# An output store that waits for a two-tap transfer to land, in a dynamic convolution with a tanh-shrink MLP behind it

## The chip, the cores and the metric

One core of one Trainium2 chip. The metric is device time in microseconds of one execution of the whole kernel, from inputs in HBM to the output in HBM. Engines are named TensorE (PE in the profile), VectorE (DVE), ScalarE (ACT), GpSimd (POOL) and SyncE (SP, which here only issues transfers).

## What is computed

The reference, cut to what matters. A softmax over 7 taps gives each token and head its own short filter; the filter runs causally over x; the result goes through two matrix products with `h - tanh(h)` between them.

```python
# x (8, 4096, 192), weight_gen (8, 4096, 8 heads, 7 taps), w_in (192, 2048), w_out (2048, 192), all float32
w = exp(weight_gen - max); w = w / sum(w)                     # over the 7 taps
x_pad = concatenate([zeros(B, 6, D), x], axis=1)              # causal: 6 rows of zeros ahead
x_unf = x_pad[:, idx, :].reshape(B, S, 7, H, D // H)
conv = einsum('bshk,bskhg->bshg', w, x_unf).reshape(B * S, D)
h = conv @ w_in
out = (h - tanh(h)) @ w_out                                   # (32768, 192)
```

## The kernel before, in words

The 32768 tokens are cut into 32 groups of 1024 tokens (128 partitions by 8 tokens). Everything is written out by hand in program order (a manual schedule); each engine runs its own instructions in that order and waits on semaphores for what it needs. The main loop runs over **bodies** n = 1 to 31. A body has 16 steps, f = 0 to 15, and does for different groups at once:

- TensorE: the first product of group n (`gemm1(n, f)`, line 584, tile `ph`), the second product of group n-1 in pieces (`out_pairs`, line 653, tiles `obank`), and in steps 13 and 14 the transposes of group n+1 (`transposes` and `conv_sums`, line 524, tile `pc`), which also add up those tap products that are still separate.
- ScalarE: tanh (line 597), the copies of finished output blocks to `out_sb` (`store_out`, line 672; two buffers), the exponentials (line 202).
- VectorE: `h - tanh(h)` (line 598, tile `gt`), and the small softmax work.
- GpSimd: the tap products of group n+2 (`products`, line 297). Taps 0 to 3 go into tile `pa` (three buffers), taps 4 to 6 into tile `pb` (one buffer).

The taps are added up by accumulating transfers from SBUF to SBUF that GpSimd issues (`dma_sum`, line 286). For groups 10 to 31 there are two: the **first sum** adds `pb`'s three taps to three of `pa` (`pa<-pb`, 1152 KB). Then the **second sum** adds taps 2 and 3 of `pa` to taps 0 and 1 (`pa<-pa`, 768 KB), the two-tap transfer of this case. The transposes then read only taps 0 and 1. GpSimd's order is: first sum of group m, `pa` products of group m+1, second sum of group m, `pb` products of group m+1, first sum of group m+1, and so on. The second sum of group n+1 comes in body n, in `products(n + 2)`, which is called at f = 1.

`LOCKED` names groups whose first sum has a further condition: its place in the program is step `LOCK` = 10 of the body two ahead of its group (`rest()`, line 954), and it waits for VectorE's subtraction of that step (`last_sub`).

SyncE issues the rest in program order, one queue: in body n the load of x for group n+3 (line 172, into `x_ring`; 1344 KB for an even group, 768 KB for an odd one), which waits until GpSimd has read the old rows; the **output store** of group n-2 (line 676, 768 KB), whose last block is finished by ScalarE at the end of f = 1; in bodies 9, 13, 17, 21 and 25 a small transfer that writes 6 rows of zeros at a sequence's start (line 182, `x_ring<-zero`, 4.5 KB), which waits for the x load of that body; and the load of weight_gen for group n+5 (line 161, 224 KB), which the exponential in body n+1 reads. From body 9 on the x load stands ahead of the store in the program.

A transfer's landing raises a semaphore, and whoever reads its bytes waits for that on its own engine. `order(inst, other, reason)` (line 144) makes one instruction wait for another, where `other` may be a transfer: then the wait is for its landing.

Of the kernel before, what the change touches and what calls it, by code (L numbers as in the profile page):

```python
# [16 lines left out]
def kernel(  # L17
# [8 lines left out]
    nc = tc.nc  # L26
# [25 lines left out]
    EXTRA_NORM = False  # L52

    WG_AT = 11
    LOCK, LOCKED = 10, tuple(range(15, 32))
    WARM = 0
    SUM_LATE = ()
    SUM_BEHIND = ()
# [19 lines left out]
    X3_AT = 3  # L78
    X3_BEHIND = None
    HALF = ()  # L80
    WOUT_CAST = ()
    SKEW = 6
    TAPS1 = ((True, 0, 1, 0, 8), (True, 1, 2, 0, 8), (False, 4, 6, 0, 8), (False, 6, 7, 0, 8), (False, 2, 4, 0, 8))
# [56 lines left out]
    tap_of = {}  # L140
    pace_of = {}
    sum_of = {}

    def order(inst, other, reason):
        tc.add_manual_dep(
            inst.ins,
            other.ins.name,
            mybir.DependencyInfo(mybir.DependencyClass.Sync, mybir.DependencyReason.DATA),
            reason=reason,
        )  # L150
# [3 lines left out]
    def tokens(t, n):  # L154

        m = n // 2
        return t[2 * m * TOK : 2 * (m + 1) * TOK].rearrange("(p s j) ... -> p s j ...", p=P, j=J)[:, n % 2]
# [127 lines left out]
    def dma_sum(out, in_):  # L285
        return nc.gpsimd.dma_start(  # L286
            out=out.rearrange("p k j d -> p k (j d)"),
            in_=in_.rearrange("p k j d -> p k (j d)"),
            accum_op=mybir.AluOpType.add,
            max_dma_last_dim=2 * J * D,  # L290
        )
# [65 lines left out]
    def products(n, taps=None, sums=None, hooks={}):  # L357
# [28 lines left out]
        def parts(*ks):  # L386
            return [[prod(k, k + 1)[:, 0] for k in ks]] * NC
# [27 lines left out]
        for k0, k1 in zip(cuts, cuts[1:]):  # L415
            if n - 1 in SUM2_EARLY and k0 == end - 1:
                second_sum(n - 1)
            m = most(k0, k1)
            if first is None and n - 1 in sum_of:
                sum_of.pop(n - 1)()  # L420
            first = first or m
        x_after[n + 1] = first
        second_sum(n - 1)
        def rest():
            a = PART_FILL.get(n, 0)
# [14 lines left out]
            else:  # L440
# [19 lines left out]
                if n in TWO_SUMS:  # L460
                    to_sum[n] = pa
                    prods_of[n] = parts(0, 1)
                elif n in HALF:
                    to_sum[n] = pa
# [3 lines left out]
                if n == NTOT - 1:  # L468
                    second_sum(n)
                    third_sum(n)  # L470
# [9 lines left out]
    def second_sum(n):  # L480

        if n in to_sum:
            pa = to_sum.pop(n)
            pairs = 1 if n in HALF else 2
            dma_sum(pa[:, 0:pairs], pa[:, 2 : 2 + pairs])
            if n in THREE or n in SINGLE:
                whole[n] = pa

# [150 lines left out]
    def out_stream():  # L639

        for i in range(LAST + 1):
            ops = []
            for r, blk in ((0, i), (1, i - 1)):
                if not 0 <= blk < LAST:
                    continue
                n, j = divmod(blk, J)
                if r == 0:
                    half[blk] = obank[blk % 2]
                ops.append((r, n, j, half[blk]))
            for f in range(NFT):  # L650
                for r, n, j, po in ops:
                    col = (j % 2) * HT + (j // 2) * P
                    mm = nc.tensor.matmul(  # L653
                        po[:, 0:D],
                        lhsT=g_of[n][f][r * R : (r + 1) * R, col : col + P],
                        rhs=w_out[r * R : (r + 1) * R, f, :],
                        start=(r == 0 and f == 0),
                        stop=(r == 1 and f == NFT - 1),
                    )
                    if r == 1 and f == 0 and i in (1, LAST):  # L660
                        order(mm, probe[0] if i == 1 else last_act[0], "row tiles in one bank")
                if f == NFT - 1 and i > 0:
                    store_out(i - 1)
                yield

    def store_out(blk):
        n, j = divmod(blk, J)
        po = half.pop(blk)
        if j == 0:
            out_of[n] = opool.tile([P, J, D], FP32, name="out_sb")  # L670
        out_sb = out_of[n]
        last_act[0] = nc.scalar.activation(out=out_sb[:, j, :], in_=po[:, 0:D], func=ACT.Copy)  # L672
        if j == J - 1:
            out_of.pop(n)
            g_of.pop(n)
            nc.sync.dma_start(
                out=tokens(out, n),
                in_=out_sb[:],
            )

    pairs = out_stream()

# [132 lines left out]
    if SOFT_EARLY:  # L815
# [6 lines left out]
        sums=SUMS1,  # L822
        hooks={} if WOUT_CAST else {6: load_w_out},
    )
# [202 lines left out]
```

## Time and profile before

| | us |
|---|---|
| median of 3 runs | 738.52 (738.18, 738.52, 741.08) |
| the profiled execution | 740.38 |
| its span, first to last instruction | 738.5 |
| TensorE busy | 716.7 (97%) |
| VectorE busy | 681.1 (92%) |
| GpSimd busy | 660.6 (89%) |
| ScalarE busy | 636.7 (86%) |
| mean granted clock of TensorE | 0.994 |

All times in the profile count from the span's start. A line of the timeline reads: start, duration, engine, line, operation, out<-in, and in brackets the idle time of the engine ahead of it and what ended it. In a line of waits stand the total, the number and the longest. In a row of windows stand the stretch, its length, each engine's busy time with its number of instructions, the granted clock of TensorE (1.00 is full), the share of the 16 DMA engines that was busy, and GB/s. In the DMA view q0 is GpSimd's queue and q1 is SyncE's, with packets, MB and share of the engines' time; a line of issues ends with the median time from issue to landing.

### The profile page before, as it was taken

What the parts mean: (1) busy time and instruction counts of PE and PEld (TensorE: products, weight loads), DVE (VectorE), ACT (ScalarE), POOL (GpSimd) and SP (SyncE); (2) the same over time, 40 slices, a digit from 0 to 9 for tenths busy, and PEclk for the clock granted to TensorE, in tenths of its full rate; (3) what the DMA queues carried; (4) which work ended last, traced back from release to release, by engine and by line L of the source; (5) the groups of instructions that cost most, each with busy time, mean ns of one, the idle gap of its engine ahead of it and who ended that gap; (6) DMA issues with size and microseconds to landing.
All of it is one profiled execution on the core that took longest, in us unless ns stands there. A gap on an engine that the chain in (4) does not pass through costs nothing.

```text
span 738.5 us, 29769 instructions
## 1 busy us (share of the span) xinstructions
PE 716.7 (97%) x13472; PEld 551.1 (75%) x13472; DVE 681.1 (92%) x718; ACT 636.7 (86%) x871; POOL 660.6 (89%) x170
## 2 busy tenths in 40 slices
PE   3799999999998999999999999999999999999998
PEld 2477777777776777777777777777777777777777
DVE  7999999999998899999999999999999999988883
ACT  4888888988887889988989989898998999888882
POOL 7999999999999999989999999999999999996000
PEclk9999999999999999999999999999999999999999
DMA  7745276765558887766987878798786889766312
GB/s 203 163 101 162 101 188 142 184 177 122 136 145 206 199 227 168 175 158 171 233 206 172 191 147 206 179 236 197 157 185 160 207 197 216 172 140 110 88 45 87
DMA packets 35053, 122.97 MB, mean 167 GB/s; under 512 B 4607, under 2 KB 9455, under 8 KB 33006
## 3 DMA queue, kind: packets, MB, share of 16 engines
q0 software_dynamic: 20208, 53.48, 41.7%
q1 hardware_dynamic: 14718, 67.59, 26.1%
q8 instruction: 105, 1.72, 0.9%
q14 instruction: 22, 0.18, 0.1%
HBM read 45.08 MB, written 25.17 MB: 95 GB/s over the span
## 4 chain that ended last, share of the span: by engine, by line
PE 88%; DVE 4%; POOL 4%; DMA 2%; issue 1%; ACT 1%; POOLq 0%; DVEq 0%
PE obank L653 42%; PE ph L584 41%; PE pc L524 4%; POOL pa L297 2%; DVE gt L598 2%; PE po L697 1%; DMA pa<-pa 1%; POOL pb L297 1%; DVE pa L297 1%; DVE pb L297 0%; DMA wg_t<-in_weight_gen_dram 0%; ACT th L597 0%; POOL pa L286 0%; DVE obank L256 0%; DVE zsum L216 0%
## 5 line engine op out<-in xcount | busy, mean ns | idle before, releaser
L598 DVE TENSOR_TENSOR gt<-ph,th 128x1024 bf16<-128x1024 f32 x512 | 598.6, 1218 | 36.5 <-ACT th L597 29.7
L597 ACT ACTIVATE th<-ph 128x1024 f32<-128x1024 f32 x512 | 513.0, 1027 | 67.0 <-PE ph L584 52.8
L584 PE MATMUL ph<-convT,w_in 64*128 64x512 bf16 x3072 | 413.5, 378 | 4.6 <-DVE gt L598 3.6
L653 PEld LDWEIGHTS <-gt 64*128 64x128 bf16 x7936 | 354.0, 94 | 84.3 <-issue 12.4
L653 PE MATMUL obank<-w_out,gt 64*128 64x192 bf16 x7936 | 407.2, 243 | 0.1
L297 POOL TENSOR_TENSOR pa<-x_ring,wsm 128x3072 bf16<-128x3072 f32 (+2 forms) x73 | 346.1, 5008 | 0.2
L297 POOL TENSOR_TENSOR pb<-x_ring,wsm 128x4608 bf16<-128x4608 f32 (+4 forms) x34 | 286.3, 8423 | 2.2 <-DVE wsm L279 1.2
L584 PEld LDWEIGHTS <-w_in 64*128 64x128 bf16 x3072 | 159.8, 94 | 80.1 <-issue 12.8
L672 ACT ACTIVATE out_sb<-obank 128x192 f32<-128x192 f32 x248 | 81.7, 329 | 9.5 <-PE obank L653 8.3
L550 ACT ACTIVATE convT<-pc 128x1024 bf16<-128x1024 f32 (+1 forms) x62 | 50.7, 820 | 5.9 <-PE pc L524 5.6
L286 POOL DMA_DIRECT2D pa<-pa x24 | 39.5, 1648 | 8.3 <-DMA pa<-pb 8.0
L286 POOL DMA_DIRECT2D pa<-pb x28 | 37.3, 1333 | 10.4 <-POOL pb L297 6.7
L524 PEld LDWEIGHTS <-pa 64*128 64x128 bf16 x1920 | 39.2, 100 | 9.3 <-POOL pb L297 3.0
L524 PE MATMUL pc<-ident,pa 64*128 64x64 bf16 x1824 | 38.6, 191 | 4.1 <-DMA pa<-pa 2.5
L216 DVE TENSOR_REDUCE zsum<-wg_t 128x32 f32<-128x224 f32 (+1 forms) x61 | 23.6, 388 | 3.0 <-ACT wg_t L202 3.0
L202 ACT ACTIVATE wg_t<-wg_t 128x448 f32<-128x448 f32 x32 | 18.2, 569 | 6.8 <-DMA wg_t<-in_weight_gen_dram 6.8
L279 DVE TENSOR_TENSOR wsm<-wg_t,pc 128x448 f32<-128x448 f32 x27 | 16.8, 621 | 2.5
L297 DVE TENSOR_TENSOR pa<-x_ring,ph 128x384 bf16<-128x384 f32 x30 | 16.6, 554 | 1.3
L243 DVE RECIPROCAL pc<-zsum 128x64 f32<-128x64 f32 x27 | 14.8, 549 | 0.0
L524 PE MATMUL pc<-ident,pb 64*128 64x64 bf16 x216 | 4.9, 206 | 9.3 <-POOL pb L297 9.3
L524 PEld LDWEIGHTS <-pb 64*128 64x128 bf16 x288 | 6.3, 107 | 9.8 <-POOL pb L297 9.3
L697 PE MATMUL po<-w_out,gt 64*128 64x192 bf16 x256 | 11.9, 243 | 0.0
(26 smaller groups left out, 55.1 us busy)
## 6 DMA issues: line engine op xcount, KB each, us to landing
pa<-pb POOLq DMA_DIRECT2D x28, 1152.0 KB, 9.7
out_dram<-out_sb SPq DMA_DIRECT2D x31, 768.0 KB, 4.1
x_ring<-in_x_dram SPq DMA_DIRECT2D x15, 1344.0 KB, 8.3
pa<-pa POOLq DMA_DIRECT2D x24, 768.0 KB, 8.4
x_ring<-in_x_dram SPq DMA_DIRECT2D x17, 768.0 KB, 5.3
wg_t<-in_weight_gen_dram SPq DMA_DIRECT2D x32, 224.0 KB, 6.0
w_out<-in_moe_w_out_dram POOLq DMA_DIRECT2D x1, 768.0 KB, 9.7
out_dram<-out_sb SPq DMA_DIRECT2D x4, 192.0 KB, 3.5
```

What stands on the lines that cost most here:

```text
L202: last_exp[0] = nc.scalar.activation(out=wg_t[:].rearrange("p j h k -> p (j h k)"), in_=wg_t[:].rearrange("p j h k -> p (j h k)"), func=AC ...
L216: nc.vector.reduce_sum(out=zsum_of[n][:, j0 * H : j1 * H], in_=e_of[n][:, j0:j1].rearrange("p j h k -> p (j h) k"), axis=AX.X,)
L286: return nc.gpsimd.dma_start(out=out.rearrange("p k j d -> p k (j d)"), in_=in_.rearrange("p k j d -> p k (j d)"), accum_op=mybir.AluOpTyp ...
L297: return eng.tensor_mul(bass.AP(tensor=out.tensor, offset=out.offset + j0 * D, ap=[out.ap[0], [J * D, nk], [G, run], [1, G]]), bass.AP(ten ...
L524: nc.tensor.matmul(pc[r][:, col : col + R] if home else pc[:, r, col : col + R], lhsT=prods[c][gi][r * R : (r + 1) * R, 2 * j : 2 * j + 2] ...
L550: last_conv[0] = nc.scalar.activation(out=out, in_=pc[:, :, 0:cols].rearrange("p r (cj t) -> p r cj t", t=R), func=ACT.Copy,)
L584: nc.tensor.matmul(ph[:, r, :], lhsT=w_in[r * R : (r + 1) * R, c, ff], rhs=convT[r * R : (r + 1) * R, c, :], start=(c == 0), stop=(c == NC ...
L597: last_act[0] = nc.scalar.activation(out=th[:], in_=ph_f, func=ACT.Tanh)
L598: last_sub[0] = nc.vector.tensor_sub(gt[:], ph_f, th[:])
L653: mm = nc.tensor.matmul(po[:, 0:D], lhsT=g_of[n][f][r * R : (r + 1) * R, col : col + P], rhs=w_out[r * R : (r + 1) * R, f, :], start=(r == ...
L672: last_act[0] = nc.scalar.activation(out=out_sb[:, j, :], in_=po[:, 0:D], func=ACT.Copy)
L697: nc.tensor.matmul(po[:, r, 0:D], lhsT=g_of[n][f][r * R : (r + 1) * R, col : col + P], rhs=w_out[r * R : (r + 1) * R, f, :], start=(f == 0 ...
```

## The change

Two edits. The store of group n, for n from 5 to 30, gets a wait for the landing of the second sum of group n+3, where that sum has already been issued in program order. Second sums exist for groups 10 to 31, and that of group n+3 is written in body n+2 at f = 1, just ahead of the store of group n; so the stores of groups 7 to 28, in bodies 9 to 30, get the wait. And group 14 is added to the groups whose first sum is locked to step 10.

```diff
-    LOCK, LOCKED = 10, tuple(range(15, 32))
+    LOCK, LOCKED = 10, tuple(range(14, 32))
...
+    STORE_BEHIND = tuple(range(5, 31))
...
+    second = {}
...
         if n in to_sum:
             pa = to_sum.pop(n)
             pairs = 1 if n in HALF else 2
-            dma_sum(pa[:, 0:pairs], pa[:, 2 : 2 + pairs])
+            second[n] = dma_sum(pa[:, 0:pairs], pa[:, 2 : 2 + pairs])
...
-            nc.sync.dma_start(
+            dma = nc.sync.dma_start(
                 out=tokens(out, n),
                 in_=out_sb[:],
             )
+            if n in STORE_BEHIND and n + 3 in second:
+                order(dma, second[n + 3], "order of the transfers")
```

## The prediction

> **What bounds the kernel now.** I read the page's busy shares first (TensorE 97%, GpSimd 89%), then the waits. After the first 40 us TensorE has one wait in the whole execution:
>
> ```profile
> PE pc L524 <- DMA pa<-pa: 2.5, 1, 2.5
> ```
>
> The timeline around it (start, duration, instruction) shows it in body 9, where the transposes of group 10 need that group's second sum:
>
> ```profile
> 222.10 0.33 SPq L172 DMA_DIRECT2D x_ring<-in_x_dram  x1
> 222.53 1.25 SPq L676 DMA_DIRECT2D out_dram<-out_sb  x1
> 227.11 1.72 POOL L286 DMA_DIRECT2D pa<-pa  x1
> 232.07 0.70 SPq L182 DMA_DIRECT2D x_ring<-zero  x1
> 238.14 0.74 PE L524 MATMUL pc<-ident,pa 64*128 64x64 bf16 x32 [2.52 <-DMA pa<-pa]
> ```
>
> TensorE was out of work at 235.62; the sum, issued at 227.11, landed at 238.0. The windows from store to store (us, TensorE busy, ..., granted clock) price the body, and finer ones its clock:
>
> ```profile
> 221.90:248.10 26.20, 23.68 (x404) 18.01 (x402) 21.04 (x23) 20.13 (x29) 25.90 (x7) 0.93 0.90 212
> 248.10:270.05 21.95, 21.95 (x404) 16.95 (x401) 21.04 (x23) 19.72 (x28) 21.65 (x6) 1.00 0.77 182
> ```
> ```profile
> 238.50:242.00 3.50, 3.50 (x54) 2.79 (x47) 0.00 (x0) 1.54 (x2) 3.50 (x2) 0.51 0.82 143
> ```
>
> With the same 404 matmuls body 9 is 4.25 us longer than body 10: 2.52 of waiting, and 1.73 more busy time, since right after the wait the clock is at half speed for 3.4 us. The bodies behind it have TensorE busy throughout, some 21.75 us each. So the transfers of the steady bodies cost nothing today; only body 9 can be won.
>
> Why did that sum take 10.9 us? The DMA view of 224:231, and then the landing in body 9 against body 29:
>
> ```profile
> q1 hardware_dynamic: 251, 2.02, 93.9%
> q0 software_dynamic: 24, 0.02, 2.3%
> ```
> ```profile
> pa<-pa POOLq DMA_DIRECT2D x1, 768.0 KB, 10.9
> ```
> ```profile
> pa<-pa POOLq DMA_DIRECT2D x1, 768.0 KB, 7.1
> ```
>
> In those 7 us SP's queue (the 1344 KB load and the 768 KB store, both issued earlier) holds the engines, and GpSimd's queue moves 0.02 MB: what was queued first goes first. The same order shows in 222:224, where the load and store are issued but only GpSimd's 1152 KB sum moves (q1 has no packet). In body 29 no load precedes the sum and the store is done: 7.1.
>
> **The change, part by part.** *The store's wait* (stores 7 to 28, bodies 9 to 30; second sums exist for groups 10 to 31). In body 9 the store leaves the front of the queue. The load alone: in body 11 it ran without the store from 267.4 to 271.5, 4.1 us; here it would begin at 224.4, when the engines become free, and end at 228.5. The first packets of the sum in body 29 came 2.35 us after its issue, so here at 229.5, after the load. Then it lands as in body 29: 227.11 + 7.1 = 234.2, which is 1.4 before 235.62. The wait goes entirely: 2.52 us, and with it the half clock, 1.71 (3.41 us at half speed).
>
> What is queued behind the waiting store on SP: the zero rows (x_ring<-zero, bodies 9, 13, 17, 21, 25) and the weight_gen load. Nothing else: the next x load waits for GpSimd anyway (409.6 us of SP's waits are that), about 19 us after the store's place.
>
> - The weight load: was issued at 232.87, now about 234.3 + 0.3 to 1.3 (store) + 0.8 (zero rows), at the latest 236.4. It took 5.4 to land, so 241.8; Exp reads it in body 10, at 247.29 less the gain of 4.2, 243.1. Cover 1.3 us. In body 17, by today's times, 403.02 + 7.1 + 1.3 + 5.4 = 416.8 against Exp at 421.57, less the 2 us or so by which TensorE gains on GpSimd (4.23 less the 2.39 at the lock, below): 2.7. Cost nothing; if the cover went, ScalarE and then TensorE would wait for the rest.
> - The store's own landing (4.1 in body 11): about 239; ScalarE writes that buffer again a body later. Nothing.
> - The next first sum (pa<-pb) is issued 10.4 us after the second one and moves its first packet 1.8 later. The store, 2 us of transfer, falls between 7.5 and 10.5 us after the second sum's issue: idle time of the engines today (the DMA view of 413:415 shows one packet). Nothing.
> - The zero rows must land before GpSimd's next products, 11.2 us after the second sum's issue (227.11 to 238.32; 403.02 to 414.23). Their landing isn't in the trace. Upper bound 6.2: issued at 232.07, and the products at 238.32 didn't wait. Lower bound: nothing. The nearest row is the smallest store that was timed, 192 KB in 3.5. With it: 7.1 + 0.1 + 0.4 + 3.5 = 11.1, in time by 0.1, except that body 9's store may again take 1.25 to issue (0.8 late). I take zero to 0.8 us of GpSimd in body 9. What is late next is group 11's sum: issued at 248.79, lands 7.1 later at 255.9, and TensorE, 4.25 earlier, wants it at 261.55 - 4.25 = 257.3. Slack 1.4, so the 0.8 is hidden. From there on the slack grows by 0.07 a body (TensorE 21.76, GpSimd 21.69).
>
> *Group 14 in LOCKED*: its first sum, and the products behind it on GpSimd, wait for the subtraction of f = 10 in body 12, some 12.7 us after the store's place (326.33 - 313.58 in body 13), so 304.5 against 302.56 now. That is 2 us of GpSimd's idle time taken in body 12 in place of the 2.39 that it spends at the same lock in body 13; with TensorE 4 us earlier the lock opens before GpSimd comes and does nothing. Zero both ways.
>
> **Sum.** Profiled execution: 740.38 (span 738.5) - 2.52 - 1.71 = 736.15. The median of the three runs is 738.52, 1.86 below the profiled one, and the three are 738.18, 738.52 and 741.08: two levels, apart by more than the clock's 1.71. I read the lower level as executions in which the wait didn't bring the half clock. Then they lose the wait alone: 738.52 - 2.52 = **736.0**. That is a choice: the trace shows one execution. What the trace has for it: the clock's steps lie on one raster of 3.41 us (16.69, 20.10, 238.55, 241.97); the wait of 235.62 to 238.14 lay wholly inside one interval of it, and would have been split over two had the raster lain elsewhere. Early on, 2.30 us without a matmul in 13.30:16.60 brought a step down and 1.55 us in 20.20:23.50 brought none, so a wait of 2.52 steps the clock down in some positions of the raster and not in others.
>
> The Trainium skill (TensorE: Matmul & The Clock Gate, Part 1) says the window of 3413 ns is free-running, which agrees with that raster; it also says the clock falls after at least one idle window of about 3.4 us, and by that a wait of 2.52 would cost no clock at all and the gain would be 2.5 in every execution. The row of 238.50:242.00 differs from it.
>
> **Rivals.**
> 1. *The median runs lose the clock too.* For: the profiled execution does. Against: it is 1.86 slower. 738.52 - 4.23 = 734.3. Chance 0.30.
> 2. *The wait only shrinks, or comes back smaller in body 10.* The load alone may slow beside other traffic, or GpSimd's 0.8 may grow past the slack of 1.4; or the change doesn't take the store out of the sum's way at all. For: second sums in bodies 13 to 28 took 7.5 to 10.3. Against: all of these had a load and a store issued ahead of them, and bodies 29 and 30, with no load, took 7.1 and 7.0. Keeping 1 to 2.5 of the 2.52: 737 to 738.5. Chance 0.17.
> 3. *Slower: the zero rows come too late.* Place: GpSimd's products in bodies 9, 13, 17, 21, 25, behind the wait on SP. At their upper bound of 6.2 they land 13.8 after the second sum's issue, 2.6 past 11.2: five times 13 us, less slack of 1.4 and 17 x 0.07: 10.4 us on TensorE, so 736.0 + 10.4 = 746.4, and more with half clocks. It loses the whole gain of 2.5 from 5 s - 2.6 = 2.5, that is s = 1.0, zero rows landing 4.6 after issue. Against: 3.5 for 42 times the bytes. Chance 0.12.
>
> **How the numbers follow.** The forecast, 736.0 +- 0.8, has 0.41. The line of 0.5% (3.7 us, about what a measurement of this kernel can tell from no change) lies at 734.8. Rival 1 is faster by it mostly (0.27 of 0.30), and the forecast's lower edge adds 0.09: faster 0.36. Slower: rival 3 beyond 742.2, 0.11. The rest, 0.53, is within. Range: rival 1 less 0.5 up to rival 2's end, 733.8 to 738.6; it leaves out rival 3 and some edges.
>
> **What would show it.** Right: no TensorE wait at L524 after 40 us; body 9 at 22 us from store to store with the clock at 1.00; group 10's sum landing in 7 to 7.5 us; SP's store waiting on DMA pa<-pa from body 9 on, issued some 7 us after the second sum; GpSimd's waits for zero rows under 1 us. Wrong: a wait on x_ring<-zero over 1 us in five bodies (rival 3), Exp waiting for wg_t, or the wait on pa<-pa back in body 10 (rival 2).

## The result

The changed kernel takes 736.5 us (median of 9 runs, 735.9 to 737.18) against 739.04 for the kernel before (9 runs, 738.18 to 741.08): ratio 0.9966, 95% interval 0.9955 to 0.9977, so 2.5 us or 0.34% faster; the forecast was 736.0 +- 0.8. A second measurement, beside the last kernel below, gave 736.39, ratio 0.9962 (0.9949 to 0.9975). The profiled execution took 735.9, with a span of 734.1 (740.38 and 738.5 before) and a mean granted clock of 1.000.

Body 9 in the timeline of the changed kernel (start, duration, instruction; the line numbers are shifted by 2):

```profile
222.40 0.33 SPq L174 DMA_DIRECT2D x_ring<-in_x_dram  x1
227.41 1.72 POOL L288 DMA_DIRECT2D pa<-pa  x1
234.38 0.34 SPq L678 DMA_DIRECT2D out_dram<-out_sb  x1
234.81 0.70 SPq L184 DMA_DIRECT2D x_ring<-zero  x1
235.62 0.91 SPq L163 DMA_DIRECT2D wg_t<-in_weight_gen_dram  x1
235.47 0.65 PE L526 MATMUL pc<-ident,pa 64*128 64x64 bf16 x32
238.62 5.44 POOL L299 TENSOR_TENSOR pa<-x_ring,wsm 128x2688 bf16<-128x2688 f32 x1
```

The store went out at 234.38, when the sum had landed. The transposes start at 235.47 with no bracket behind them: TensorE didn't wait. The landing in the DMA view of 227:228, and body 9 and body 10 in the windows from store place to store place (length, busy times, granted clock):

```profile
pa<-pa POOLq DMA_DIRECT2D x1, 768.0 KB, 6.9
```
```profile
221.90:243.85 21.95, 21.95 (x406) 16.89 (x404) 21.06 (x23) 19.84 (x29) 21.65 (x7) 1.00 0.84 203
243.85:265.60 21.75, 21.75 (x402) 16.80 (x400) 20.84 (x23) 19.52 (x28) 21.45 (x7) 1.00 0.77 177
```

The sum takes 6.9 in place of 10.9. Body 9 has the length of the others at full clock, 21.95 against 26.20. In the list of waits the line of TensorE for pa<-pa is gone. In the DMA section of the page the median landing of all second sums shows what the other 21 waiting stores do (the kernel before first, then the changed one):

```profile
pa<-pa POOLq DMA_DIRECT2D x24, 768.0 KB, 8.4
```
```profile
pa<-pa POOLq DMA_DIRECT2D x24, 768.0 KB, 7.1
```

### The profile page after: what moved, and what is told of

The parts are those of the page before. It is cut to its first block, busy times and chain, and to the rows that moved or that the text cites. A ratio compares the mean times of both kernels' runs of the same rounds, so it can differ in the third digit from the quotient of the medians.

```text
span 734.1 us, 29774 instructions
## 1 busy us (share of the span) xinstructions
PE 715.7 (97%) x13472; PEld 549.6 (75%) x13472; DVE 681.0 (93%) x718; ACT 636.3 (87%) x871; POOL 660.6 (90%) x170
## 4 chain that ended last, share of the span: by engine, by line
PE 94%; DVE 4%; ACT 1%; issue 0%; DMA 0%; DVEq 0%
PE obank L655 45%; PE ph L586 44%; PE pc L526 4%; DVE gt L600 2%; PE po L701 1%; DVE pa L299 1%; DVE pb L299 0%; DMA wg_t<-in_weight_gen_dram 0%; ACT th L599 0%; DVE obank L258 0%; DVE zsum L218 0%; DVE wsm L281 0%; ACT wg_t L204 0%; DVE obank L281 0%; ACT convT L544 0%
```

## The experiments

Each kernel differs from the changed one by the diff shown (`...` stands for code left out, and words behind # are notes), and is compared with runs of the kernel before on the same chip.

**Store 7 alone.**

```diff
-    LOCK, LOCKED = 10, tuple(range(14, 32))
+    LOCK, LOCKED = 10, tuple(range(15, 32))
-    STORE_BEHIND = tuple(range(5, 31))
+    STORE_BEHIND = (7,)
```

> Only store 7 (body 9) waits for the second sum of group 10; group 14 is not locked. Theory (the whole gain is TensorE's one wait in body 9, and the half clock that sometimes follows it): same time as the changed kernel, 736.5 +- 0.5, no TensorE wait on pa<-pa, clock near 1.00. Rival (the other 21 waiting stores bring part of the gain by taking traffic off the sums of the steady bodies): 737 to 738.5.

Measured: 738.29 (12 runs), ratio 0.9993 (0.9980 to 1.0005). The theory that everything is won in body 9 fell. Body 9 had no wait, but two bodies on, in body 11, there is a new one. The timeline of body 11 (SyncE, GpSimd, TensorE) and the landing:

```profile
267.78 1.12 SPq L678 DMA_DIRECT2D out_dram<-out_sb  x1
272.40 1.72 POOL L288 DMA_DIRECT2D pa<-pa  x1
282.54 0.65 PE L526 MATMUL pc<-ident,pa 64*128 64x64 bf16 x32 [1.29 <-POOL pb L299]
```
```profile
pa<-pa POOLq DMA_DIRECT2D x1, 768.0 KB, 10.1
```

The bracket names GpSimd's `pb` product, which was the last to report before. The transposes don't read it (in body 9 of the changed kernel they started at 235.47, and that product ran on to 237.5), and 272.40 + 10.1 = 282.5 is the moment at which they start, so the wait is for the sum. TensorE, no longer held in body 9, has come nearer to GpSimd. The store, which follows TensorE, is now issued 4.6 us ahead of the sum where it was 0.4 (270.05 against 270.47), the sum takes 10.1 in place of 8.8, and it no longer fits. The mended theory: body 9's wait was also what gave the later bodies their slack, the time between a sum's landing and its use. In the changed kernel the distance from a second sum's issue to its use is 257.24 - 249.09 = 8.15 in body 10 and 409.74 - 401.14 = 8.6 in body 17, where it was 261.55 - 248.79 = 12.8 and 414.06 - 403.02 = 11.0. So the whole gain is kept only while the sums land within 8.2 to 8.6 us.

**All stores but 7; the lock alone; all stores without the lock.**

```diff
-    STORE_BEHIND = tuple(range(5, 31))
+    STORE_BEHIND = tuple(range(8, 31))      # first kernel
+    STORE_BEHIND = ()                       # second kernel: the lock of group 14 alone
...
-    LOCK, LOCKED = 10, tuple(range(14, 32))
+    LOCK, LOCKED = 10, tuple(range(15, 32)) # third kernel: all stores wait
```

> Stores 8 to 28 wait, store 7 does not; group 14 is locked. Theory: the time of the kernel before, 739.0 +- 0.5, with the 2.5 us wait of TensorE in body 9 as before; among its runs those whose granted clock is near 0.995 are about 1.7 us longer than those near 1.00. Rival (steady bodies bring part): 736.5 to 738.3.

> No store waits; group 14 alone is added to the locked groups. Theory: the time of the kernel before, 739.0 +- 0.5; GpSimd idles some 2 us at its first sum of group 14 in body 12, and no longer in body 13. Rival (the lock spaces the transfers and is a part of the gain): 736.5 to 738.3. Its runs also give pairs of clock and span, as the one above.

> All 22 stores wait, group 14 is not locked. Theory: as the changed kernel, 736.5 +- 0.5. Rival (the lock is needed to keep GpSimd's transfers off the delayed stores): 737.5 or more.

Measured: all but store 7, 738.1, ratio 0.9993 (0.9978 to 1.0009); the lock alone, 738.54, 0.9993 (0.9981 to 1.0005); all stores without the lock, 736.37, 0.9964 (0.9950 to 0.9978). By these medians nothing is won that can be told from noise without store 7's wait, with all stores everything, and the lock does nothing either way. With the lock alone GpSimd's idle time moves as costed, to 2.05 us in body 12 (its timeline):

```profile
304.88 1.28 POOL L288 DMA_DIRECT2D pa<-pb  x1 [2.05 <-DVE gt L600]
```

In these two kernels store 7 and body 9 are as in the kernel before, so they give two more samples of TensorE's wait there: 2.18 us (the lock alone, a sum of 10.6) and 1.67 (all but store 7, a sum of 10.0). The line of the transposes and the window behind it, the lock alone first:

```profile
238.46 0.76 PE L526 MATMUL pc<-ident,pa 64*128 64x64 bf16 x31 [2.18 <-DMA pa<-pa]
```
```profile
238.80:242.20 3.40, 3.40 (x51) 2.69 (x45) 0.00 (x0) 1.37 (x2) 3.40 (x2) 0.50 0.74 128
```
```profile
237.82 0.65 PE L526 MATMUL pc<-ident,pa 64*128 64x64 bf16 x32 [1.67 <-POOL pb L299]
```
```profile
237.90:241.30 3.40, 3.40 (x97) 2.82 (x97) 1.00 (x2) 2.51 (x4) 3.18 (x2) 1.00 0.44 76
```

After 2.18 us the clock is halved, after 1.67 it is not. (The bracket of 1.67 again names the `pb` product; the sum, issued at 227.72, landed at 237.7.)

**Which stores.**

```diff
-    STORE_BEHIND = tuple(range(5, 31))
+    STORE_BEHIND = tuple(range(7, 31, 2))
```

> As the changed kernel, but only the stores of odd groups wait, those in bodies 9, 11, ... 29, where the x load of 1344 KB stands ahead of the second sum. Theory, mended after the run with store 7 alone (there TensorE waited 1.29 us in body 11, for a sum that took 10.1): once body 9's wait is gone, TensorE leaves each later body only 8.2 to 8.8 us from the second sum's issue to its use, so each sum must land in that time. With the store ahead, sums took 8.6 to 10.3 in odd bodies and 7.5 to 8.5 in most even ones (9.3 in body 12). So the odd stores are nearly all that is needed: 736.5 to 737.3, at most one wait, of up to 0.9 us, in body 10 or 12. Rival (any store left ahead brings the wait back in full): 738 to 739.

Measured: 737.06, ratio 0.9968 (0.9955 to 0.9980), with one wait of TensorE, in body 12, for a sum that took 9.0:

```profile
301.66 0.65 PE L526 MATMUL pc<-ident,pa 64*128 64x64 bf16 x32 [0.26 <-DMA pa<-pa]
```

The mended theory holds: body 12 is one of the two that it named, and the wait is within the 0.9 us that it allowed. What the even stores are worth, about 0.4 us, the table below shows; the medians are too close to tell.

**Released at the sum's issue.** The stores wait for GpSimd's product that stands just ahead of the second sum.

```diff
+    last_mul = {}
...
-            m = most(k0, k1)
+            last_mul[0] = m = most(k0, k1)
...
-            second[n] = dma_sum(pa[:, 0:pairs], pa[:, 2 : 2 + pairs])
+            second[n] = last_mul[0]
+            dma_sum(pa[:, 0:pairs], pa[:, 2 : 2 + pairs])
```

> The stores wait for GpSimd's product that stands just ahead of the second sum, so they are released about when the sum is issued (226.7 in body 9) and not when it lands. Theory (what is queued first goes first, and SyncE's transfers start within 1 us of issue where GpSimd's take 2.35): the store's packets still go ahead of the sum's; the sum of group 10 lands at 236 to 238, TensorE waits 1 to 2.5 us for it, 737.5 to 739. Rival (it is enough to move the store out of the x load's time; store and sum then share the engines evenly): the sum lands by 235.5 and the time is 736.5.

Measured: 738.14, ratio 0.9989 (0.9978 to 1.0000): most of the gain is gone. TensorE waited 1.35 us in body 9. The timeline of body 9 (SyncE, GpSimd, TensorE) and the DMA views of 229:231.3 and 231.3:236.5 (q1 is SyncE's queue):

```profile
228.53 0.34 SPq L680 DMA_DIRECT2D out_dram<-out_sb  x1
227.95 1.72 POOL L289 DMA_DIRECT2D pa<-pa  x1
237.54 0.65 PE L528 MATMUL pc<-ident,pa 64*128 64x64 bf16 x32 [1.35 <-DMA pa<-pa]
```
```profile
q1 hardware_dynamic: 126, 0.76, 84.5%
```
```profile
q0 software_dynamic: 269, 0.78, 84.3%
q1 hardware_dynamic: 174, 0.27, 16.2%
```

The store was issued 0.6 after the sum and still went first: in 229:231.3 its queue moved 0.76 MB, and the sum's queue had no packet at all. The sum took 9.4. So the wait has to be for the landing: a release at the issue still lets the store in ahead.

**The slower rival, forced.** The zero rows wait for the landing of the store (first kernel); and the same with the weight_gen load issued ahead of them (second kernel).

```diff
-            nc.sync.dma_start(              # the zero rows
+            dma = nc.sync.dma_start(
...
+            if n >= 12:
+                order(dma, last_store[0], "zero rows behind the store")
...
+            last_store[0] = dma             # behind the store
...
+                if n >= 9:
+                    weights(n)              # second kernel only
                 halo_of.pop(n + 3)()
```

> As the changed kernel, but the zero rows of bodies 9, 13, 17, 21 and 25 wait for the store's landing, some 3.8 us later than now. Theory (zero rows land about 3 us after issue, now just in time): GpSimd waits 3.5 to 4 us for them in each of the five bodies, 18 us in all; TensorE's slack of 1.4 us and 0.07 a body hides 2.6 of it, so TensorE waits for second sums again, 12 to 15 us in all, and half clocks may add 1 to 7: 748 to 758. Rival (GpSimd makes up the lateness, since its products are off the path): 736.5 to 738.

> As the kernel whose zero rows wait for the store's landing (758.0), but in the bodies with zero rows the weight_gen load is issued ahead of them. In that kernel ScalarE's Exp waited 17.9 us in five waits for the weight load behind the zero rows. If those waits were its cost: back to 737 to 741, with GpSimd waiting 6 to 12 us for zero rows in all, most of it hidden. If the cost was the zero rows themselves (products of GpSimd late, then second sums late): 748 or more still, with TensorE waiting at its transposes for pa<-pa.

Measured: 758.04, ratio 1.0263 (1.0228 to 1.0298), and 761.38, ratio 1.0298 (1.0271 to 1.0325). The first time lies at the upper end of what was expected (748 to 758), but for another reason. Its list of waits (total, times, longest; the profiled execution, 751.7, is the fastest of its four):

```profile
ACT wg_t L207 <- DMA wg_t<-in_weight_gen_dram: 17.9, 5, 5.3
PE obank L658 <- ACT out_sb L677: 10.3, 3, 4.7
POOL pa L302 <- DMA x_ring<-zero: 6.6, 4, 2.4
POOL pa L302 <- PE ph L589: 6.0, 1, 6.0
```

The last two are GpSimd's five late starts in the bodies with zero rows, 12.6 us in all (in body 9 the bracket names another engine, at the same place). Yet no wait of TensorE for pa<-pa is in its list. The weight load stands behind the zero rows, Exp waited for it, ScalarE's copies stood behind Exp, and TensorE waited for those. Two of Exp's five waits, 6.6 us, belong to the first 10 us and are in the changed kernel too; the other three, 11.3 us, come a body after late zero rows, each with one of TensorE's three waits behind it. The second kernel, whose weight load is in time, shows the rival itself:

```profile
PE pc L529 <- DMA pa<-pa: 18.9, 6, 5.0
POOL pa L302 <- DMA x_ring<-zero: 14.7, 3, 5.8
POOL pa L302 <- issue: 6.3, 1, 6.3
POOL pa L302 <- PE ph L589: 5.7, 1, 5.7
```

The last three are GpSimd's five late starts, all in the bodies with zero rows, 26.7 us in all; 18.9 of it reach TensorE as waits for second sums, and the clock falls to a mean of 0.986. The kernel's span, 761.6, is 27.5 above the changed kernel's.

**The store behind the weight load**, and the same without the lock, beside the changed kernel once more.

```diff
-            dma = nc.sync.dma_start(                 # at the end of f = 1
...
+            def store():                             # the same store, with its wait
...
+                late.append(store)                   # if it is one that waits
...
             if f == WG_AT:
                 weights(n)
+                while late:
+                    late.pop(0)()
```

> As the changed kernel, but on SyncE's queue the waiting store stands behind the zero rows and the weight_gen load, so that these two no longer wait for the second sum. Theory (both land in time in the changed kernel, and what waits behind the store costs nothing): 736.5 +- 0.5. Rival (their lateness holds GpSimd and ScalarE back a little in every body): 735 to 736. The weight load, now ahead of the sum again, takes some 0.6 us of the engines: sums land in 7.5 to 8.2, still in time.

> The changed kernel itself, beside the next one on the same chip. Theory: 736.5 +- 0.5. It is here so that the store behind the weight load (735.97 in another comparison) can be set against it directly.

> The waiting store stands behind the zero rows and the weight_gen load, and group 14 is not locked: the candidate for a faster version. Theory (TensorE has no wait left that this could take away): the same as the changed kernel beside it, within 0.5. Rival (the 0.5 between 735.97 and 736.5 is real): 0.5 to 1 below it.

Measured: 735.97, ratio 0.9961 (0.9947 to 0.9974); then 736.39 for the changed kernel, 0.9962 (0.9949 to 0.9975), and 737.08 without the lock, 0.9974 (0.9963 to 0.9984). The intervals overlap: what waits behind the store in the changed kernel costs nothing that shows, and no version here is faster than it.

**The loop without the start.** The traces separate the kernels better than the medians do. No edit acts before body 9, so the time from the transposes in body 8 (line of `pc<-ident,pa`) to those in body 30 holds all that the edits change. In the changed kernel these start at 215.92 and 692.59:

| profiled execution | us | above the changed kernel | waits of TensorE in it |
|---|---|---|---|
| before | 481.01 | 4.34 | 2.52, then half clock |
| changed | 476.67 | | none |
| store 7 alone | 478.26 | 1.59 | 1.29 |
| all but store 7 | 478.47 | 1.80 | 1.67 |
| the lock alone | 480.65 | 3.98 | 2.18, then half clock |
| all stores without the lock | 476.68 | 0.01 | none |
| odd stores | 477.11 | 0.44 | 0.26 |
| released at the sum's issue | 478.13 | 1.46 | 1.35 |
| store behind the weight load | 476.62 | -0.05 | none |
| the same without the lock | 476.67 | 0.00 | none |

Each loss is the wait, 0.1 to 0.3 us beside it, and 1.7 where the half clock follows. The executions also differ ahead of the loop: body 8's transposes start anywhere from 215.81 to 217.82. That is as much as most of these effects. So the higher median of the last kernel (737.08) has no cause in its loop, as far as its one traced execution shows.

## Why the prediction was right, step by step

- *Only body 9 is lost, 2.52 us of wait and 1.7 of clock.* Right for the kernel before: body 9 went from 26.20 to 21.95.
- *The sum lands 7.1 after its issue once the store is away.* Measured 6.9. The load's packets ended near 228.5, as forecast, and in the DMA view of 229:234.5 the sum moves 0.79 MB and SyncE's queue has one packet.
- *The executions of the median lose the wait without the half clock.* This was the choice that placed the forecast at 736.0 and not at 734.3. The medians differ by 2.54 us (739.04 and 736.5) where 2.52 was forecast, but the closeness is partly luck. Body 9's loss is not one number: the three profiles with that body unchanged lost 4.34 and 3.98 us with the half clock and 1.80 without it, and the wait itself went from 1.67 to 2.52. In 29 runs of the kernel before beside the first four experiments, 17 show a granted clock of 0.999 or more; an interval at half clock costs 1.71 of 737 us and would show as 0.998 or less. The median of the 17 is 738.38, which is 2.0 above the 736.37 measured beside them for all stores without the lock; that of the other 12 is 740.16. So the executions without the half clock seem to lose about 2 and the others about 4, and the median of both kinds came to 2.5. This is not proved: where in those 12 the half clock fell is not recorded (the profile of before has one at 16.69 to 20.10 too), and the 17 alone range from 737.27 to 740.45. The profiled execution, which had the half clock in body 9, gained 4.4 us of span, as rival 1 has it.
- *What is queued behind the store costs nothing.* Right: the weight load was issued at 235.62 and landed by 238.7, against Exp at 242.97. The zero rows, for which the row of 3.5 was taken, were issued at 234.81, and the products that need them began at 238.62, 0.82 after the first sum's issue as before. No GpSimd time was lost in body 9, where zero to 0.8 were allowed for.
- *The slack in body 10 is 1.4.* Measured 8.15 - 6.9 = 1.25.
- *The lock is worth zero both ways.* Shown: with all stores waiting, the loop without it differs by 0.01 us.
- *Rival 3.* Its mechanism is real; it needs zero rows that are later than they are. Its sum left out what stands behind them, the weight load, whose time to spare was used up first when the zero rows were made late.
- What the prediction didn't say: that the 21 other waiting stores are needed. It read the bodies behind body 9 as free of cost, which they were only with the 4 us that body 9 lost. Its own term for body 10, a use at 257.3 and a sum of 7.1, took the wait of that body's store for granted; with the sums of the profile before, the same working (a use 4.25 earlier) leaves nothing to spare in body 11 (8.8 us from issue to use, a sum of 8.8) and is 0.4 short in body 12 (8.85 against 9.3). With store 7 alone the wait did come back in body 11, and larger. The forecast held because the change makes all the stores wait, for which the prediction named no need: there its number was lucky.

## What to carry to other kernels

A single stall can be what keeps the rest of a pipeline comfortable: before claiming it, subtract it from the slack of every later stage, and see which of them then needs the same treatment. To keep a transfer out of another's way, hold it until the other has landed; a release at the other's issue is too early where the other's packets start later. And price a forced wait by everything that stands behind it on its queue, down to the last small load.

## What the runs showed of the hardware

- Transfers of two queues mostly went one after the other here, in the order in which their packets were ready: 0.76 MB of the store ahead of a sum issued 0.6 us before it. In 222.9:224 of the kernel before, the x load issued at 222.10 had no packet beside 62 of the first sum's, though the x loads issued at 36.50 and 58.42, with nothing else in flight, had packets after about 1 us. The Trainium skill (DMA: Bandwidth & Descriptors, Queues, rings and completion order) has the engines take turns between queues packet by packet; the stretch of 224:231 before the change (93.9% against 2.3%) differs from that, since by the 2.35 us of body 29 the sum's packets could have started about 229.5, and the measurement decides. But small transfers did move beside a sum: with the release at the sum's issue, 0.27 MB of SyncE's queue (the weight load, mostly) in 231.3:236.5, beside 0.78 of the sum. What decides between the two, no run here shows.
- Waits of TensorE of 2.52 and 2.18 us were followed by 3.4 us at half clock, waits of 1.67, 1.35 and 1.29 by none. The Trainium skill (TensorE: Matmul & The Clock Gate, Part 1) gives one idle window of about 3.4 us as the condition; here less was enough. But the length alone doesn't decide. In the first kernel with late zero rows a wait of 2.93 us was followed by full clock:

```profile
607.84 1.50 PE L658 MATMUL obank<-w_out,gt 64*128 64x192 bf16 x32 [2.93 <-ACT out_sb L677]
```
```profile
607.80:611.20 3.40, 3.33 (x58) 2.51 (x59) 2.62 (x4) 3.22 (x5) 3.40 (x2) 1.00 0.35 145
```

The clock's steps in that execution (15.96, 19.37, 248.06, 428.97, 432.38) lie on one raster, whole multiples of 3.41 us apart, as the prediction read it in its own trace. Carried on, the raster has a point at 606.46, which splits this wait (604.91 to 607.84) into 1.55 and 1.38 us. The wait of 2.67 us there (426.50 to 429.17) had 2.47 us ahead of the point at 428.97 and was followed by half clock. So it is the idle time inside one interval that counted here: 1.55 us brought no step, 2.18 did.
- The zero rows, 4.5 KB, took at most 3.8 us behind the store on their own queue, with nothing of GpSimd's queue moving (234.81 to 238.62). Issued at 239.46, behind a first sum issued at 238.11, they held GpSimd until 245.65: 6.2 us. That the sum in flight is what made them slower fits this and was not tested by itself.
